# Moving the split of a streamed chunk later in the engines' order, in a kernel of Infini-attention beside a Fourier mixing layer

## The chip, the cores and the metric

The kernel runs on one core of one Trainium2 chip. The metric is the device time of one execution in microseconds (us). Three timed runs of the kernel before gave 1032.37, 1034.28 and 1035.39; the median is 1034.28.

## What is computed

Two independent layers, laid side by side in the output (2048 rows, 576 + 576 columns, float32):

```python
def _A_ref(x, wq, wk, wv, wo, beta):        # 32 heads of 18, 4 segments of 512
    ...
    for s in range(N):
        p = _softmax(qs @ ks^T * scale + mask)       # causal, inside the segment
        o = g * (phi(qs) @ M / (phi(qs) @ z)) + (1 - g) * (p @ vs)
        M, z = M + phi(ks)^T @ vs, z + sum(phi(ks))
    return o @ wo

def _B_ref(x, dft_seq_re, dft_seq_im, dft_hid_re, dft_hid_im):
    a = x @ dft_hid_re^T
    b = x @ dft_hid_im^T
    return dft_seq_re @ a - dft_seq_im @ b
```

(The first function is shortened to its mathematics.) The second layer, B, is the one that matters here: a product with a 576 x 576 matrix, and then one with a 2048 x 2048 matrix, once for the real and once for the imaginary part.

## The kernel before

To come near float32 in TensorE's fast formats, an operand is split into a high part and a low part: ScalarE copies it into the fast format (`hi`), and another engine subtracts that from the original (`lo`). A product is then hi·hi + hi·lo + lo·hi.

**Stages.** Up to about 230 us the projections of layer A run (L435 to L479). From there to about 960 us attention (`attention`, L811) and layer B (`dense`, L579) are woven together: attention is a list of slots, eight to each of 68 steps, and after every slot the loop at L879 takes pieces from the generator `dense` until layer B has come as far, by a planned share of time, as attention has. At each slot `tick` (L84) is called first; it runs what `later(n, ...)` (L81) has put off by n slots. The order in which instructions are written is the order in which each engine executes them: the schedule is manual, every engine takes its own list in order, and a waiting instruction holds up all behind it on its engine. From 960 us to the end there is the output projection (L899).

**Chunks of layer B.** The operands that layer B streams from memory come in 160 chunks (L369): for each of the two parts `ri`, 16 chunks of x (`xtT`, 128 x 640 values, one to each `hidden` at L536) and then 64 chunks of the 2048 x 2048 matrix (`cT`, 128 x 512 values, four to each `sequence` at L555). A chunk has three steps in its life:

- `c_load(n)` (L372): a DMA on SP's queue into `craw`, one of 4 buffers.
- `c_cut(n)` (L380): ScalarE writes `chi` (L387), for an x chunk also `xtail` (L389), from `craw` into one of 3 buffers; one slot later (L395) GpSimd writes `clo` (L392, and L394 for the tail). The first two chunks are cut in the stage before, with VectorE in GpSimd's place (L475).
- TensorE multiplies with `chi` and `clo` as weights: 28 matmuls to an x chunk (L545 to L550), 24 to a chunk of the matrix (L499).

`chunk(n)` (L531) is called when TensorE's order comes to chunk n. It issues the load of chunk n + 4 and the cut of chunk n + 2, and hands out the tiles of chunk n.

`sequence` walks through 16 steps `so`, four to a chunk. `product` (L495) takes the first two steps together, twelve steps singly, and the last two together again (`EDGE`, L493): a step's instructions written inside `steps` (L569) stand ahead of that step's matmuls.

**Others on the same queues.** On SP: loads of keys and queries (L426), the transposing DMA of the scores (L715), loads of y (L529). On ScalarE: the exponentials of the scores (L699, L754, L755), which also free the two pairs of PSUM banks that score matmuls (L670, L744 to L751) fill. On GpSimd: parts of the split of the exponentials (L710, L769), and the mask (L759).

Of the kernel before, what the change touches and what calls it, by code (L numbers as in the profile page):

```python
# [24 lines left out]
NT = S // P  # L25
# [11 lines left out]
def infini_attention_and_fnet(ctx: ExitStack, tc: tile.TileContext, xT, wqk, w8, wv, wo, beta, xtT, cT, hT, out):  # L37
# [15 lines left out]
    def split(hi, lo, raw, lo_engine=None):  # L53
        act.activation(hi, raw, AF.Copy)
        (lo_engine or dve).tensor_tensor(lo, raw, hi.bitcast(F32), OP.subtract)
# [25 lines left out]
    def later(n, fn, *a):  # L81
        due.setdefault(clock[0] + n, []).append((fn, a))
# [54 lines left out]
    def wide_tile(cols):  # L137
        return lambda: wide.tile([P, cols], F32R, name="wide", tag="wide")
# [233 lines left out]
    def c_load(n):  # L372
        if n < len(CHUNKS) and n not in c_seen:
            c_seen.add(n)
            src, at, k = CHUNKS[n]
            t = sr.tile([P, 5, P], F32, name="craw", bufs=4)
            dma(t[:, :k], src[at])
            c_raw[n] = t

    def c_cut(n, engine=pool):  # L380
        if n < len(CHUNKS):
            raw = c_raw.pop(n)
            hi = sr.tile([P, 4, P], F32R, name="chi", bufs=3)
            lo = sr.tile([P, 4, P], F32R, name="clo", bufs=3)
            t = sr.tile([P, P], F32R, name="xtail", bufs=3) if CHUNKS[n][2] == 5 else None
            c_split[n] = hi, lo, t
            act.activation(hi, raw[:, :4], AF.Copy)  # L387
            if t is not None:
                act.activation(t, raw[:, 4], AF.Copy)  # L389

            def low():
                engine.tensor_tensor(lo, raw[:, :4], hi.bitcast(F32), OP.subtract)  # L392
                if t is not None:
                    engine.tensor_tensor(t[64:], raw[64:, 4], t[64:].bitcast(F32), OP.subtract)  # L394
            later(1, low)  # L395
# [99 lines left out]
    def product(steps, count, evacuate):  # L495
        o = [ps.tile([P, 288], F32, name="d", bufs=3) for _ in range(2)]

        def mm(a, b, h, start=False, stop=False):
            pe.matmul(o[h], a, b[:, h * 288:h * 288 + 288], start=start, stop=stop)  # L499

        def edge(last):
            ops = [next(steps) for _ in range(EDGE)]
            for h in range(2):
                for n, (hi, lo, m_hi, m_lo) in enumerate(ops):
                    mm(hi, m_lo, h, start=n == 0 and not last)
                    mm(hi, m_hi, h)
                    mm(lo, m_hi, h, stop=n == EDGE - 1 and last)
                if last:
                    evacuate(h, o[h])
                yield 3 * EDGE * MM  # L510

        yield from edge(False)
        for _ in range(count - 2 * EDGE):
            hi, lo, m_hi, m_lo = next(steps)
            for h in range(2):
                mm(hi, m_lo, h)
                mm(hi, m_hi, h)
            yield 4 * MM
            for h in range(2):
                mm(lo, m_hi, h)  # L520
            yield 2 * MM
        yield from edge(True)
# [3 lines left out]
    def y_load(tt):  # L526
        if tt < NT:
            Y[tt] = sb.tile([P, D], F32, name="y", bufs=4)
            dma(Y[tt], yd[tt])  # L529

    def chunk(n):  # L531
        c_load(n + 4)
        c_cut(n + 2)
        return c_split.pop(n)

    def hidden(ri, tt):  # L536
        hi, lo = [(wide_tile(D)() if tt < 11 else sb.tile([P, D], F32R, name="ab", bufs=10)) for _ in range(2)]
        AB.append((hi, lo))
        xh, xl, xt = chunk(ri * 80 + tt)
        wh, wl, wt1, wt2 = HW[ri]  # L540
        for h in range(2):
            cs = slice(h * 288, h * 288 + 288)
            o = ps.tile([P, 288], F32, name="d", bufs=3)
            for k in range(4):
                pe.matmul(o, xh[:, k], wl[k][:, cs], start=k == 0, stop=False)  # L545
                pe.matmul(o, xh[:, k], wh[k][:, cs], start=False, stop=False)  # L546
                pe.matmul(o, xl[:, k], wh[k][:, cs], start=False, stop=False)  # L547
                yield 3 * HM
            pe.matmul(o, xt, wt1[:, cs], start=False, stop=False)
            pe.matmul(o, xt, wt2[:, cs], start=False, stop=True)  # L550
            split(hi[:, cs], lo[:, cs], o)
            yield 2 * HM
        yield BREAK

    def sequence(ri, tt):  # L555
        if ri:
            y_load(tt + 1)
            y = Y.pop(tt)
        else:
            y = sb.tile([P, D], F32, name="y", bufs=4)  # L560

        def evacuate(h, o):
            cs = slice(h * 288, h * 288 + 288)
            if ri == 0:
                act.activation(y[:, cs], o, AF.Copy)
            else:
                dve.tensor_tensor(y[:, cs], y[:, cs], o, OP.subtract)

        def steps():  # L569
            for so in range(NT):  # L570
                if so % 4 == 0:
                    hi, lo, _ = chunk(ri * 80 + NT + tt * 4 + so // 4)
                yield hi[:, so % 4], lo[:, so % 4], *AB[ri * NT + so]

        yield from product(steps(), NT, evacuate)
        later(2, dma, out[tt * P:(tt + 1) * P, D:] if ri else yd[tt], y)
        yield BREAK

    def dense():  # L579
        for ri in range(2):  # L580
            for tt in range(NT):
                yield from hidden(ri, tt)
            if ri:
                y_load(0)
            for tt in range(NT):
                late = tt - 8
                if ri == 0 and 0 <= late < 5:
                    h_load(1, late)
                if ri == 0 and 1 <= late < 6:
                    h_split(1, late - 1)  # L590
                if ri and 0 <= late < 5:
                    wo_load(late)
                if ri and 1 <= late < 6:
                    wo_split(late - 1)
                yield from sequence(ri, tt)
# [303 lines left out]
    for t in range(NT):  # L899
        o_transpose(t + 1)  # L900
        hi, lo, tl = OT.pop(t)
# [47 lines left out]
```

## Time and profile before

| | |
|---|---|
| timed runs, median | 1034.28 us (1032.37 to 1035.39) |
| the profiled execution: its time | 1032.0 us |
| its span, first to last instruction | 1030.3 us |
| granted TensorE clock | 1.0 |
| 235 to 960 us (attention and layer B) | where the changed lines run |
| `chi` (ScalarE, L387) | 160 of 632 ns (median) |
| `clo` on GpSimd (L392) | 158 of 1288 ns (median) |
| loads into `craw` (SP, L377) | 128 of 256 KB and 32 of 320 KB |

How to read what follows: PE is TensorE's matmuls, PEld its weight loads, DVE VectorE, ACT ScalarE, POOL GpSimd, SP the engine that issues the DMAs. In a list of waits, a row gives the waiting engine with what it writes and the line, what it waited for, and then the total in us, the number of times and the longest. In a timeline, a row gives start, duration, engine, line, operation, tiles and shapes, and in brackets how long the engine had stood idle and who ended that. Matmuls are pipelined, so that one lasts about 300 ns while the next starts 133 ns after it.

### The profile page before, as it was taken

What the parts mean: (1) busy time and instruction counts of PE and PEld (TensorE: products, weight loads), DVE (VectorE), ACT (ScalarE), POOL (GpSimd) and SP (SyncE); (2) the same over time, 40 slices, a digit from 0 to 9 for tenths busy, and PEclk for the clock granted to TensorE, in tenths of its full rate; (3) what the DMA queues carried; (4) which work ended last, traced back from release to release, by engine and by line L of the source; (5) the groups of instructions that cost most, each with busy time, mean ns of one, the idle gap of its engine ahead of it and who ended that gap; (6) DMA issues with size and microseconds to landing.
All of it is one profiled execution on the core that took longest, in us unless ns stands there. A gap on an engine that the chain in (4) does not pass through costs nothing.

```text
span 1030.3 us, 25826 instructions
## 1 busy us (share of the span) xinstructions
PE 1006.0 (98%) x9464; PEld 940.7 (91%) x9464; DVE 719.8 (70%) x1903; ACT 713.7 (69%) x1654; POOL 625.3 (61%) x668
## 2 busy tenths in 40 slices
PE   9999999999999999999999999999999999999998
PEld 7989989899999999999998999998899888899998
DVE  6545657465678777778778777778688778896442
ACT  7657575653887878878877787876677767875333
POOL 3557575766666666767667676666566666766000
PEclk9999999999999999999999999999999999999999
DMA  7516253377768999999999988899999999968574
GB/s 265 172 65 201 88 166 145 130 234 186 166 155 195 197 211 196 213 187 211 235 192 216 207 199 165 163 211 197 205 221 214 220 217 210 243 150 192 155 209 138
DMA packets 287263, 194.26 MB, mean 189 GB/s; under 512 B 210208, under 2 KB 242336, under 8 KB 287136
## 3 DMA queue, kind: packets, MB, share of 16 engines
q1 hardware_dynamic: 287136, 192.61, 79.2%
q8 instruction: 74, 1.21, 0.5%
q14 instruction: 53, 0.43, 0.1%
HBM read 106.64 MB, written 43.78 MB: 146 GB/s over the span
## 4 chain that ended last, share of the span: by engine, by line
PE 69%; DMA 11%; ACT 6%; SPq 6%; POOL 5%; issue 2%; DVE 1%; POOLq 0%; ACTq 0%; DVEq 0%
PE d L499 21%; DMA craw<-cT 8%; PE qk L77 6%; PE d L77 6%; PE v L77 5%; PE qk L229 5%; PE s L670 4%; PE d L545 3%; PE d L546 3%; PE d L547 3%; POOL clo L392 3%; SPq L715 2%; PE pv L786 2%; SPq L87 2%; PE look L338 2%
## 5 line engine op out<-in xcount | busy, mean ns | idle before, releaser
L676 DVE CUSTOM_DVE_ANT_0 s<-s,causal 128x128 f32<-128x128 f32 (+3 forms) x512 | 251.2, 499 | 109.9 <-PE s L670 95.3
L392 POOL TENSOR_TENSOR clo<-craw,chi 128x512 fp32r<-128x512 f32 x158 | 214.1, 1356 | 125.5 <-ACT chi L387 80.4
L499 PE MATMUL d<-wide,chi 128*128 128x288 f32 x1408 | 266.5, 306 | 0.0
L499 PEld LDWEIGHTS d<-wide,chi 128*128 128x128 f32 x1408 | 212.3, 189 | 3.3 <-issue 2.2
L499 PE MATMUL d<-wide,clo 128*128 128x288 f32 x704 | 178.1, 319 | 0.0
L710 POOL TENSOR_TENSOR hl<-pf,hl 128x768 f16<-128x768 f32 x64 | 111.5, 1742 | 77.8 <-ACT hl L706 57.9
L387 ACT ACTIVATE chi<-craw 128x512 fp32r<-128x512 f32 x160 | 100.9, 631 | 63.4 <-DMA craw<-cT 40.6
L670 PE MATMUL s<-ks,qs 108*128 108x128 bf16 (+3 forms) x512 | 133.9, 304 | 10.5 <-ACT pf L699 8.4
L699 ACT ACTIVATE pf<-s,nb 128x128 f32<-128x128 f32 (+3 forms) x256 | 128.1, 526 | 6.2
L499 PE MATMUL d<-ab,chi 128*128 128x288 f32 x640 | 126.1, 306 | 0.0
L499 PEld LDWEIGHTS d<-wide,clo 128*128 128x128 f32 x704 | 119.0, 189 | 1.8 <-issue 0.9
L769 DVE TENSOR_TENSOR plo<-pf,phi 128x384 f16<-128x384 f32 (+1 forms) x128 | 110.9, 867 | 0.2
L754 ACT ACTIVATE phi<-t 128x384 f16<-128x384 f32 x128 | 62.1, 485 | 66.3 <-PE t L751 66.2
L499 PEld LDWEIGHTS d<-ab,chi 128*128 128x128 f32 x640 | 98.5, 189 | 4.4 <-issue 4.0
L755 ACT ACTIVATE pf<-t 128x384 f32<-128x384 f32 (+1 forms) x192 | 99.9, 520 | 1.3 <-PE t L744 1.3
L706 ACT ACTIVATE hl<-pf 128x768 f16<-128x768 f32 (+1 forms) x128 | 87.4, 730 | 2.0
L499 PE MATMUL d<-ab,clo 128*128 128x288 f32 x320 | 84.9, 314 | 0.0
L545 PE MATMUL d<-wide,chi 128*128 128x288 f32 x256 | 84.3, 329 | 0.0
L546 PE MATMUL d<-wide,chi 128*128 128x288 f32 x256 | 75.6, 295 | 0.0
L547 PE MATMUL d<-wide,clo 128*128 128x288 f32 x256 | 75.5, 295 | 0.0
L710 DVE TENSOR_TENSOR hl<-pf,hl 128x512 f16<-128x512 f32 x64 | 72.1, 1127 | 1.8 <-ACT hl L706 1.8
L769 POOL TENSOR_TENSOR plo<-pf,phi 128x384 f16<-128x384 f32 x64 | 62.4, 976 | 11.1 <-ACT pf L755 10.6
(196 smaller groups left out, 2510.4 us busy)
## 6 DMA issues: line engine op xcount, KB each, us to landing
craw<-cT SPq DMA_DIRECT2D x128, 256.0 KB
ks<-kd SPq DMA_DIRECT2D x192, 72.0 KB
qs<-qd SPq DMA_DIRECT2D x192, 72.0 KB
craw<-xtT SPq DMA_DIRECT2D x32, 320.0 KB
out<-y SPq DMA_DIRECT2D x31, 288.0 KB
vd<-vs SPq DMA_DIRECT2D x16, 440.0 KB
vst<-vd SPq DMA_DIRECT2D x32, 220.0 KB
qd<-p SPq DMA_DIRECT2D x16, 384.0 KB
```

Source lines behind the costliest of these rows:

```text
L77: pe.matmul(o, a, b, start=n == 0, stop=n == len(terms) - 1)
L387: act.activation(hi, raw[:, :4], AF.Copy)
L392: engine.tensor_tensor(lo, raw[:, :4], hi.bitcast(F32), OP.subtract)
L499: pe.matmul(o[h], a, b[:, h * 288:h * 288 + 288], start=start, stop=stop)
L545: pe.matmul(o, xh[:, k], wl[k][:, cs], start=k == 0, stop=False)
L546: pe.matmul(o, xh[:, k], wh[k][:, cs], start=False, stop=False)
L547: pe.matmul(o, xl[:, k], wh[k][:, cs], start=False, stop=False)
L670: pe.matmul(o[:, c:c + w], q[:, i * P:w], k[:, :w], start=True, stop=True)
L676: dve.tensor_tensor_reduce(o[:, c:c + w], o[:, c:c + w], CAUSAL[0][:, L - w:], scale=scale, scalar=-LOWEST, op0=OP.add, op1=OP.min, accum_ ...
L699: act.activation(f[:, FIRST_COL[i]:FIRST_COL[i] + w], o[:, c:c + w], AF.Exp, bias=nb[:, i:i + 1], scale=-1.0)
L710: engine.tensor_tensor(hl[:, 1, a:b], f[:, a:b], hl[:, 0, a:b], OP.subtract)
L769: (pool if kind == 2 else dve).tensor_tensor(lo[:, a:b], f[:, a:b], hi[:, a:b], OP.subtract)
```

## The change

The cut of chunk n + 2 no longer stands in `chunk(n)`. In `hidden` it is written after the first half of the chunk (14 of 28 matmuls and the split of their result); in `sequence` it is written when the chunk's fourth step is taken. The load of chunk n + 4 stays in `chunk(n)`. `c_cut` itself, the number of buffers and all amounts of work are as before.

```diff
     def chunk(n):
         c_load(n + 4)
-        c_cut(n + 2)
         return c_split.pop(n)
...
             split(hi[:, cs], lo[:, cs], o)
+            if h == 0:
+                c_cut(ri * 80 + tt + 2)
             yield 2 * HM
...
             for so in range(NT):
+                n = ri * 80 + NT + tt * 4 + so // 4
                 if so % 4 == 0:
-                    hi, lo, _ = chunk(ri * 80 + NT + tt * 4 + so // 4)
+                    hi, lo, _ = chunk(n)
+                if so % 4 == 3:
+                    c_cut(n + 2)
                 yield hi[:, so % 4], lo[:, so % 4], *AB[ri * NT + so]
```

## The prediction

> **What bounds the kernel now.** I read the page's busy shares first, then the busy time by stretch, then the waits of TensorE, and then the two lines that the change moves.
>
> ```profile
> PE 1006.0 (98%) x9464; PEld 940.7 (91%) x9464; DVE 719.8 (70%) x1903; ACT 713.7 (69%) x1654; POOL 625.3 (61%) x668
> ```
>
> TensorE is the bound, and 1030.3 - 1006.0 = 24.3 us of the span is its idle time. No change to ScalarE or GpSimd can win more than that unless matmuls get denser. The stretches say where the idle time is (columns: window, length, busy us and count of PE, PEld, DVE, ACT, POOL, granted clock, DMA share, GB/s):
>
> ```profile
> 300.00:400.00 100.00, 99.28 (x1088) 93.01 (x1088) 77.87 (x228) 78.49 (x187) 67.45 (x73) 1.00 0.93 196
> ...
> 500.00:600.00 100.00, 96.92 (x1048) 90.49 (x1047) 78.53 (x220) 78.53 (x189) 68.95 (x70) 1.00 0.96 208
> 600.00:700.00 100.00, 99.98 (x1047) 94.36 (x1046) 76.83 (x233) 78.71 (x196) 67.35 (x80) 1.00 0.91 182
> 700.00:800.00 100.00, 95.43 (x1038) 89.17 (x1037) 77.94 (x227) 72.54 (x170) 63.64 (x66) 1.00 0.97 212
> 800.00:900.00 100.00, 94.02 (x1012) 87.46 (x1011) 80.60 (x222) 73.45 (x167) 66.77 (x69) 1.00 1.03 223
> ```
>
> 300-400 and 600-700 have under 1 us of idle TensorE; 500-600 has 3.1, 700-800 4.6, 800-900 6.0. From 235 to 960, where the changed lines run, it comes to 17.5 us. TensorE's own waits name who ends it; these are all of them in 232-960:
>
> ```profile
> PE s L670 <- ACT pf L699: 8.4, 10, 1.6
> PE t L747 <- ACT pf L699: 3.4, 4, 1.5
> PE trm L727 <- ACT pf L755: 1.8, 4, 0.7
> PE s L670 <- DVE negm L676: 1.6, 2, 0.9
> PE t L744 <- DMA qs<-mt: 1.5, 1, 1.5
> ```
>
> ScalarE's exponentials (L699, L755) free the score banks that TensorE wants next: 8.4 + 3.4 + 1.8 = 13.6 us. The 1.5 us on the maxima's DMA is ScalarE's too: the tile `mt` is written by ScalarE (L729). Together 15.1 us. ScalarE is busy only 73-79% in these stretches, so it is late because it was blocked, and the moved line says by what (idle time of ScalarE just before `chi`, and who waited for `chi`):
>
> ```profile
> its engine sat idle before it (us, times) until:
>   DMA craw<-cT: 40.6, 29
>   DMA craw<-xtT: 8.3, 3
>   PE t L744: 7.0, 2
>   PE d L499: 3.6, 6
>   PE t L751: 1.7, 1
>   PE pv L787: 1.0, 1
>   issue: 0.7, 1
> who waited for it (us, times):
>   POOL clo L392: 80.4, 65
> ```
>
> The sum is 62.9 us. One case from the timelines of ScalarE and TensorE:
>
> ```profile
> 711.42 0.63 ACT L387 ACTIVATE chi<-craw 128x512 fp32r<-128x512 f32 x1 [4.50 <-DMA craw<-cT]
> ...
> 714.42 0.69 ACT L699 ACTIVATE pf<-s,nb 128x512 f32<-128x512 f32 x1
> ```
> ```profile
> 714.35 0.38 PE L670 MATMUL s<-ks,qs 108*128 108x512 bf16 x1 [1.52 <-ACT pf L699]
> ```
>
> The load of this chunk is issued on SP at 706.83, and `chi` waits for it until 711.4. Exponentials stand behind it in ScalarE's order, and TensorE stops 1.52 us for one of them. I went through the 19 gaps of TensorE in 235-960 that are put to ScalarE or to `qs<-mt`: all but one (0.70 us, at 922.7) have such a wait of `chi` in the 5 us before them. So **14.4 of the 17.5 us** of idle are the price of `chi` waiting for its load in ScalarE's queue.
>
> **The change, part by part.** No instruction is added or removed: 160 `chi` (L387, 632 ns median), 32 `xtail`, 158 `clo` on GpSimd (L392, 1288 ns median) stay. Only their place in the two queues moves. The loads are issued at the same place in SP's order, so SP's queue (192 `ks`, 192 `qs`, 160 `craw`, 64 transposes and the rest) keeps its order.
>
> *How far it moves.* In the trace's order a cT chunk has 24 main matmuls of TensorE. The split moves from ahead of the first to ahead of the 19th; in the last chunk of a row (steps 14 and 15 are fetched together, L502) to ahead of the 13th. In an xtT chunk it moves to behind the 14th of 28. By the trace's times of those matmuls: 3.2, 2.2 and 2.0 us, median of all 3.0. In the xtT chunk it also stands behind ScalarE's evacuation of the first half (L551, 0.41 us a piece), which waits for that 14th matmul; `clo` of the chunk two ahead keeps 2.7 us or more there once the start is over, so this costs nothing. A cT chunk lasts 4.5 us, an xtT chunk 4.9.
>
> *The load's lead.* Where `chi` waited, it started 4.6 us (median) after its load was issued. From the load's issue to TensorE reaching the old place there are 5.5 us in the median, and under 4.6 us in 54 of 153 chunks (the first seven left out). To the new place there are 8.3 us, and under 4.6 us in 6 of 153, short by 4.2 us in all six together. A wait of `chi` under about 1 us is followed by no gap on TensorE. I take 1 us of TensorE's 14.4 as left: **-13.4 us**. Bounds: 0, if a later load always eats the lead, and -15.1, all of ScalarE's.
>
> [...]
>
> *The wait for TensorE.* `chi` of chunk n+2 takes the buffer of chunk n-1 (3 buffers, L383). At the head of chunk n that chunk has only just ended (`PE d L499: 3.6, 6`); 3 us on it has long ended. Nothing waits on that 3.6 us but ScalarE, so I count no gain beyond the above.
>
> *What is shortened: the lead of `clo` before TensorE.* From the head of chunk n to the end of `clo` of n+2 takes 3.7 us in the median (ScalarE's lag, 0.63 us of `chi`, the tick to the next slot, 1.3 us of `clo`); the first matmul that reads it comes 9.7 us after the head. That leaves 5.9 us. Taking away each chunk's own shift leaves 3.0 us in the median. If each lag is kept as it was, waits for loads included, only two chunks fall short: chunk 2 by 0.6 us, chunk 54 by 0.02. If lags of chunks without a load wait are set against all leads, the shortfall sums to 1.0 us. I take **+1.6 us** (1.0 and chunk 2's 0.6). Bounds: 0, and for the other end see the first rival. TensorE's waits of before show `PEld d L499 <- POOL clo L392` just once (1.2 us).
>
> *Buffers of the load.* The load of n+4 reuses the buffer that `clo` of n releases (4 buffers, L376). It is issued at least 3.5 us after that release now; with the shift at least 0.3, median 6.1. SP gets no new wait, and what stands behind it (transposes, `ks`, `qs`) is not held up. Price 0; if SP ran ahead of its place by more than 6 us, a load would wait and with it the transposes.
>
> *What is late next.* Each `chi` wait also holds up GpSimd's `clo` (80.4 us, 65 times), the score split behind it, and SP's transpose, which waits 84.0 us for `clo`; behind that transpose stands the next load (the load at 706.83 was issued right after a transpose that had held SP 3.9 us). Removing the wait loosens that loop; I count nothing for it. VectorE is at 77-81% and holds TensorE up only twice (1.6 us).
>
> Sum: -13.4 + 1.6 = **-11.8 us** on the profiled 1032.0 us, so 1020.2. The profiled run lies 2.3 us under the median of the three timed runs, 1034.28; from that the change gives 1022.5. I predict **1022.5**.
>
> **The rivals.**
>
> *Slower: TensorE waits for `clo`.* The 3.0 us left for `clo` must cover all that GpSimd has ahead of it. If the new place falls such that each `clo` stands behind one more score split (L710, 1742 ns), the leads of the trace fall short by 21 us in all; at 1.36 us more lag they fall short by 12.7, which is the turning point against 13. Then 1034.3 - 13.4 + 21 = 1042. For it: 61% busy on GpSimd, and a lag that can't be seen at the new place. Against it: chunk heads already fall at all phases of the slots, so the lags seen now contain such queues, and 32 of them hold a load wait that goes.
>
> [...]
>
> *The wait moves on, half the gain.* With `chi` out of the way ScalarE's next waits or VectorE's score minima set the banks, as in the two gaps put to VectorE. If half of the 13.4 comes back, the time is 1034.3 - 6.7 + 1.6 = 1029.
>
> *The transfers are the bound.* The DMA share is 0.96-1.03 just where TensorE idles and 0.91-0.93 where it doesn't. If loads are late because the engines are full, a longer lead fills up again and nothing is won: 1034. Against it: 600-700 runs without idle TensorE at 0.91, so the loads' pace suffices there with little to spare, and the waits are single ones of up to 4.5 us behind a held SP queue, not a lag that grows.
>
> *It doesn't do what it says:* the split would have to stay ahead of the chunk's first matmul in ScalarE's order; nothing in the code makes it.
>
> **How the numbers follow.** Forecast (1015 to 1028) 0.62; half the gain (1026 to 1032) 0.14; transfers or no effect (1032 to 1037) 0.09; slower by late `clo` (1037 to 1055) 0.15. The range takes in the first two, the bound of -15.1 with the denser loop behind it, and most of the third: 1014 to 1035, leaving out 0.15 above and a few hundredths below. About 0.3% (3 us) is what a measurement of this kernel can tell from no change. Faster 0.76, same 0.09, slower 0.15.
>
> **What would show it.** Right: idle before `chi` until `craw` falls from 48.9 us to under 10; TensorE's waits for ScalarE in 235-960 from 13.6 to under 3; 700-900 gets busier than 98%. Wrong: new rows of TensorE waiting for `clo` of more than 5 us; `chi` still waiting for `craw` 20 us or more (transfers the bound); or the `chi` wait gone with TensorE's idle unchanged under another name.

## The result, and the profile after

The changed kernel takes **1025.50 us** in the median of nine runs (1023.30 to 1032.20); the kernel before, timed beside it, 1032.37 us (nine runs). The ratio is **0.9939, with a 95% interval of 0.9913 to 0.9966**: by that ratio 6.3 us faster on 1034.28 us, where 11.8 us were forecast (the two medians, 1032.37 and 1025.50, differ by 6.9). The changed kernel's two profiles below were taken in executions of 1032.2 and 1027.0 us.

The first profile is thus of the slowest of the nine executions, with a span (first to last instruction) of 1030.5 us. The second (`e1_again`, below) has a span of 1025.3 us; its execution is 1.5 us above the median. Both are read here, since what differs between them is part of the answer.

First ScalarE's idle time just before `chi`, from the view of that line in the first profile after:

```profile
its engine sat idle before it (us, times) until:
  DMA craw<-cT: 14.0, 9
  PE d L499: 5.4, 3
  DMA craw<-xtT: 3.2, 1
  POOL mb L726: 2.0, 1
```

The waits for the load fell from 48.9 us in 32 waits to 17.2 us in 10: the change does what it says. But the waits that are left are longer, up to 6.1 us against 4.5. Rows of this view that name an engine which writes nothing that `chi` reads should be counted with them: for the chunks of `PE t` and `PE pv` before (9.6 us, 4 times), and of `POOL mb` and two of `PE d` after (4.9 us, 3 times), the load had been issued 3.9 to 6.3 us before `chi` began, as in the rows that name it, and the buffer of `chi` had been free for 1.1 to 5.0 us. By that count, an estimate, the waits for loads went from 58.5 us to 22.1, and to 18.0 in the second profile. TensorE's own waits in 232-960, same profile:

```profile
PE s L674 <- ACT pf L703: 7.4, 3, 4.6
PE t L748 <- DMA qs<-mt: 6.3, 6, 1.9
PE s L674 <- DVE negm L680: 1.1, 3, 0.7
...
```

In the second profile the first two are:

```profile
PE s L674 <- ACT pf L703: 6.6, 3, 2.8
PE t L748 <- DMA qs<-mt: 4.8, 3, 2.3
```

(L674, L703, L748 and L680 are L670, L699, L744 and L676 of before.) The waits for ScalarE's exponentials went from 18 short ones, 13.6 us, to three, 7.4 us. The DMA that brings the scores' maxima (`qs<-mt`, two transfers of 3 KB), waited for once before, 1.5 us, now costs 6.3. And the stretches show something new in the column behind the five engines, the granted clock:

```profile
700.00:800.00 100.00, 96.69 (x1048) 90.18 (x1044) 79.37 (x228) 74.42 (x172) 66.54 (x68) 1.00 0.99 212
800.00:900.00 100.00, 93.46 (x981) 87.36 (x980) 76.79 (x219) 70.02 (x161) 62.03 (x67) 0.95 1.00 219
```

In stretches of 10 us the place is seen:

```profile
830.00:840.00 10.00, 5.42 (x42) 5.13 (x41) 3.73 (x10) 4.64 (x10) 3.97 (x3) 0.66 1.03 180
...
870.00:880.00 10.00, 10.00 (x99) 9.35 (x98) 7.15 (x24) 6.19 (x17) 4.23 (x8) 0.83 1.01 201
```

TensorE had half its clock for 6.8 us from 832.8 and for 3.4 us from 870.4. The first lies inside and behind its longest stop, the second behind the stop of 1.88 us for the maxima's DMA that ended at 869.0. In 870-880 TensorE is busy throughout and still does 99 matmuls, where 820-830 holds 111. The profile of before has no such stretch from 235 to 960.

The longest stop, from the timelines of SP, ScalarE and TensorE of the same profile:

```profile
818.87 4.12 SPq L719 DMA_TRANSPOSE ptt<-hl  x1
...
828.45 0.36 SPq L377 DMA_DIRECT2D craw<-cT  x1
```
```profile
833.44 0.63 ACT L387 ACTIVATE chi<-craw 128x512 fp32r<-128x512 f32 x1 [6.13 <-DMA craw<-cT]
```
```profile
834.72 0.58 PE L674 MATMUL s<-ks,qs 108*128 108x128 bf16 x2 [4.58 <-ACT pf L703]
```

SP issues two loads of chunks 10.1 us apart (818.33 and 828.45), where TensorE at full pace uses one every 4.5 us: between them stand the transposing DMA and eight other issues. The split, though late, comes too early for that load; ScalarE stops 6.1 us and TensorE 4.6.

Adding up what TensorE's time went into (idle time in 235-960 from its gaps; half of the time at half clock, an estimate of the work lost in it: in the first profile after, L499's matmuls start 240 ns apart (median) in these stretches, and 133 ns apart at full clock from 840 to 850; the rest of the span):

| profile | span | idle | lost to half clock | rest |
|---|---|---|---|---|
| before | 1030.3 | 17.5 | 0 | 1012.8 |
| after | 1030.5 | 16.0 | 5.1 | 1009.4 |
| after, again | 1025.3 | 12.7 | 3.4 | 1009.2 |

So the idle time of 5.7 us that I expected (17.5 - 13.4 + 1.6) is 12.7 to 16.0, and 3.4 to 5.1 us go to the clock by that estimate. The rest falls by some 3.5 us: the stop of before at 714.35 cost some 0.16 us beyond its idle time (it puts 1.68 us more than usual between two starts, of which 1.52 are idle), and there are 27 stops of more than 0.06 us before, 17 and 11 after; if each cost as much, that is, by estimate, 1.6 to 2.6 us of it.

### The profile page after: what moved, and what is told of

Its sections match the earlier page's. It is cut to its first block, busy times and chain, and to the rows that moved or that the text cites. A ratio compares the mean times of both kernels' runs of the same rounds, so it can differ in the third digit from the quotient of the medians.

```text
span 1030.5 us, 25808 instructions
## 1 busy us (share of the span) xinstructions
PE 1008.0 (98%) x9464; PEld 943.8 (92%) x9464; DVE 724.8 (70%) x1903; ACT 714.6 (69%) x1654; POOL 624.8 (61%) x668
## 4 chain that ended last, share of the span: by engine, by line
PE 80%; DMA 8%; ACT 5%; DVE 3%; POOL 2%; issue 1%; SPq 1%; POOLq 0%; DVEq 0%; ACTq 0%
PE d L499 33%; PE s L674 6%; PE d L77 6%; PE qk L77 5%; PE qk L229 4%; PE v L77 4%; PE pv L790 4%; DMA qs<-mt 3%; PE d L544 2%; PE d L545 2%; PE d L546 2%; PE pv L791 2%; PE m L313 2%; PE look L338 1%; DMA ks<-kd 1%; PE t L748 1%
## 5 line engine op out<-in xcount | busy, mean ns | idle before, releaser
L680 DVE CUSTOM_DVE_ANT_0 s<-s,causal 128x128 f32<-128x128 f32 (+3 forms) x512 | 250.8, 500 | 112.1 <-PE s L674 98.8
L392 POOL TENSOR_TENSOR clo<-craw,chi 128x512 fp32r<-128x512 f32 x158 | 211.0, 1336 | 123.3 <-ACT chi L387 86.1
L499 PE MATMUL d<-wide,chi 128*128 128x288 f32 x1408 | 268.0, 307 | 0.0
L499 PEld LDWEIGHTS d<-wide,chi 128*128 128x128 f32 x1408 | 213.6, 190 | 2.6 <-issue 1.6
L499 PE MATMUL d<-wide,clo 128*128 128x288 f32 x704 | 178.7, 320 | 0.0
L714 POOL TENSOR_TENSOR hl<-pf,hl 128x768 f16<-128x768 f32 x64 | 115.9, 1811 | 70.6 <-ACT hl L710 59.2
L674 PE MATMUL s<-ks,qs 108*128 108x128 bf16 (+3 forms) x512 | 134.6, 305 | 9.2 <-ACT pf L703 7.4
L703 ACT ACTIVATE pf<-s,nb 128x128 f32<-128x128 f32 (+3 forms) x256 | 128.3, 527 | 6.2
L499 PE MATMUL d<-ab,chi 128*128 128x288 f32 x640 | 126.7, 307 | 0.0
L499 PEld LDWEIGHTS d<-wide,clo 128*128 128x128 f32 x704 | 119.6, 190 | 0.9
L773 DVE TENSOR_TENSOR plo<-pf,phi 128x384 f16<-128x384 f32 (+1 forms) x128 | 113.8, 889 | 0.0
L759 ACT ACTIVATE pf<-t 128x384 f32<-128x384 f32 (+1 forms) x192 | 100.4, 523 | 8.5 <-PE t L748 8.4
L499 PEld LDWEIGHTS d<-ab,chi 128*128 128x128 f32 x640 | 99.4, 190 | 0.4
L499 PE MATMUL d<-ab,clo 128*128 128x288 f32 x320 | 85.6, 317 | 0.0
L714 DVE TENSOR_TENSOR hl<-pf,hl 128x512 f16<-128x512 f32 x64 | 75.2, 1175 | 0.1
L773 POOL TENSOR_TENSOR plo<-pf,phi 128x384 f16<-128x384 f32 x64 | 59.7, 933 | 16.8 <-ACT pf L759 15.9
```

Source lines behind the costliest of these rows:

```text
L674: pe.matmul(o[:, c:c + w], q[:, i * P:w], k[:, :w], start=True, stop=True)
L680: dve.tensor_tensor_reduce(o[:, c:c + w], o[:, c:c + w], CAUSAL[0][:, L - w:], scale=scale, scalar=-LOWEST, op0=OP.add, op1=OP.min, accum_ ...
L703: act.activation(f[:, FIRST_COL[i]:FIRST_COL[i] + w], o[:, c:c + w], AF.Exp, bias=nb[:, i:i + 1], scale=-1.0)
L714: engine.tensor_tensor(hl[:, 1, a:b], f[:, a:b], hl[:, 0, a:b], OP.subtract)
L759: act.activation(f[:, r:r + w], o[:, :w], AF.Exp, bias=LIFT, scale=SCALE)
L773: (pool if kind == 2 else dve).tensor_tensor(lo[:, a:b], f[:, a:b], hi[:, a:b], OP.subtract)
```

## The experiments

Theory A, formed on these profiles: the gain is the load's lead, as forecast, and its remainder is eaten by the clock and by the maxima's DMA, which is a matter of order in the queues. Against it B (the clock is chance), C (the gain comes from the new place of the split on ScalarE and GpSimd and not from the load), D (the transfers are the bound) and E (the maxima's DMA is only a symptom). Each ratio is against the kernel before, run on the same chip in the same rounds.

**The changed kernel again** (no edit).

> The changed kernel once more, for a second profile and its clock. Theory A (the change takes chi's wait for its load, 48.9 us, down to about 17 us, and the rest of the expected gain is eaten by a half clock of TensorE after its longest waits and by new waits for the maxima's DMA): 0.993 to 0.995 of the kernel before; granted clock below 1 again, with each stretch at 0.5 right behind an idle time of TensorE of about 2 us or more; TensorE's waits for the maxima's DMA again above the 1.5 us of before. Rival B (the profiled run was an odd one; the clock has nothing to do with the change): the clock stands at 1.000 and the time at 0.989, as predicted.

Measured: 0.9940 (0.9919 to 0.9961). The mean granted clock of its nine runs is 0.9969; that of 32 runs of the kernel before is 0.9985. (1 - clock) times the span, the same estimate of the work lost, is 3.2 us against 1.5. By it some 1.7 us of the forecast gain went to the clock in the mean of the timed runs. B falls: none of the changed kernel's eighteen timed runs stands at 1.000, and the time is not 0.989.

**The load one chunk earlier, the split left at the head.**

```diff
     def chunk(n):
-        c_load(n + 4)
+        c_load(n + 5)
         c_cut(n + 2)
```

> The kernel before with the load issued one chunk earlier (chunk n loads n + 5 in place of n + 4) and the split left at the head. Theory A (what the change wins is the load's lead before chi): the lead grows by a whole chunk, 4.5 us, more than the change's 3.0 us, so chi's waits for craw fall below 10 us and the time to 0.988 to 0.993. Rival C (the gain comes from where the split stands in the order of ScalarE and GpSimd, not from the load's lead): 0.998 to 1.002. Rival D (the transfers are the bound): chi's waits stay above 30 us and the time within 0.3% of before.

Measured: 0.9953 (0.9931 to 0.9976), 1025.36 us in the median. `chi`, and then TensorE:

```profile
  DMA craw<-xtT: 4.2, 3
...
  DMA craw<-cT: 0.9, 1
```
```profile
PE t L744 <- DMA qs<-mt: 8.2, 6, 4.0
```

C falls: nearly the same gain comes without moving the split. D falls in the form it had here: `chi`'s waits did not stay above 30 us. But A misses its range too (0.988 to 0.993): the waits for the load are down to 5.1 us and the time is no better than with 17.2 us of them. The maxima's DMA has taken their place, with a stop of 4.0 us and 6.8 us of half clock that set in during it. In that case ScalarE had written the maxima at 832.5, SP came to their DMA at 838.2, behind a transpose and ten other issues, and TensorE went on at 843.2. So of 10.7 us, 5.7 were spent in SP's order and 5.0 after SP had come to the DMA, for 6 KB.

**Only one part of the change.** In `hidden` or in `sequence` the three lines of the old `chunk` are put back at the chunk's head:

```diff
-        xh, xl, xt = chunk(ri * 80 + tt)
+        c_load(ri * 80 + tt + 4)
+        c_cut(ri * 80 + tt + 2)
+        xh, xl, xt = c_split.pop(ri * 80 + tt)
...
-            if h == 0:
-                c_cut(ri * 80 + tt + 2)
```

(This is `e3_sequence_only`, which undoes the change in `hidden`; `e2_hidden_only` undoes it in `sequence` in the same way.)

> Only the sequence part of the change (cT chunks split late, in the fourth step; in hidden the split stays at the chunk's head). Theory A: 40.6 of the 48.9 us of waits for craw and all but two of TensorE's gaps behind such a wait lie in the cT chunks, so this has nearly the whole gain: 0.993 to 0.996. Rival C (gain spread by the number of chunks, 128 of 160): 0.995 to 0.997.

Measured: 0.9950 (0.9931 to 0.9969), inside what A and C both allow.

> Only the hidden part of the change (xtT chunks: the split behind the first half). Theory A: 8.3 us of wait for craw in three waits lie there, and TensorE lost about 1 us behind one of them (586 us); 0.998 to 1.001. Rival: by the number of chunks (32 of 160) 0.998 to 0.999, which this cannot tell apart; above 1.003 the later clo in hidden costs something.

Measured: 0.9992 (0.9966 to 1.0018). The gain is in `sequence`, where 40.6 of the 48.9 us of waits for loads were. The interval takes in both rivals' numbers; that nothing is lost in `hidden` is shown, within 0.2%.

**A shorter lead still.** The split of chunk n + 1 at the head of chunk n:

```diff
     def chunk(n):
         c_load(n + 4)
+        if n:
+            c_cut(n + 1)
...
-            if h == 0:
-                c_cut(ri * 80 + tt + 2)
...
-                if so % 4 == 3:
-                    c_cut(n + 2)
```

> The changed kernel with the split later still: that of chunk n + 1 at the head of chunk n, a lead of 1.0 chunks and not 1.25. The rival of the prediction (TensorE waits for clo): the median lead of clo falls from 3.0 to about 1.4 us, the turning point; by the leads of the trace the shortfalls then sum to some 13 us, so rows of TensorE waiting for clo or chi of 8 to 20 us and 1.000 to 1.012 of before. If leads under 3 us are harmless (the lags at the later place are shorter, since the load has landed by then): 0.992 to 0.996.

Measured: 0.9965 (0.9945 to 0.9986), 1028.22 us. TensorE's waits:

```profile
PE t L746 <- DMA qs<-mt: 4.6, 2, 2.7
PE d L499 <- POOL clo L392: 3.0, 4, 1.0
...
PE d L499 <- ACT chi L387: 0.8, 2, 0.6
```

Here the forecast's first rival appears, at less than half of the least that was expected: 3.8 us of waits for `clo` and `chi`, not 8 to 20. In this kernel `chi` waits for a load once, 0.2 us. So the leads of the trace of before overstated the risk, and a lead of 1.25 chunks is not short in this kernel.

**The maxima's DMA.** Three ways to have it earlier. First their transpose a slot earlier, on the changed kernel and on the load-early one:

```diff
+            if p % 2 == 0 and 0 < p <= NP:
+                maxima_transpose(p // 2 - 1)
             even(0, s_fill, 1)
...
-            if p % 2 == 0 and 0 < p <= NP:
-                maxima_transpose(p // 2 - 1)
             even(V_LAG, pv)
```

> The changed kernel with the transpose of the maxima, and so its two DMAs, one slot (some 1.3 us) earlier. Theory A (what ate the rest of the gain are TensorE's waits for the maxima's DMA, 4.8 and 6.3 us in two profiles of the changed kernel, and the half clock behind the longest of them): those waits fall below 3 us, and the time to 0.989 to 0.992 of the kernel before. Rival E (the maxima's DMA is a symptom: it is late because everything on SP is late behind the transposing DMAs, and something else will wait): the waits for it fall but the time stays at 0.993 to 0.995.

Measured: 1.0035 (1.0015 to 1.0055), 1037.19 us.

> The kernel before with the load issued one chunk earlier, the split left at the head, and the maxima's transpose one slot earlier. Theory A: chi waits for craw under 10 us as in the load-early kernel, and TensorE's waits for the maxima's DMA under 3 us (8.2 there): 0.987 to 0.991, granted clock 0.998 or more. Rival E: 0.994 to 0.996 as the load-early kernel alone.

Measured: 1.0050 (1.0030 to 1.0069). Both miss what either theory said, by a mistake in the experiment: the transpose needs a PSUM bank that ScalarE has not yet read at that slot. TensorE's waits in the changed kernel with this edit:

```profile
PE trm L731 <- ACT pf L759: 15.8, 10, 6.0
...
PE t L748 <- DMA qs<-mt: 0.5, 1, 0.5
```

The wait for the DMA is gone (0.5 us), and a new one, of TensorE for ScalarE's exponentials (L759), is larger than what it cured. They tell A and E apart no further. Second, the two DMAs issued by ScalarE:

```diff
-            later(1, dma, qs_bufs[G % 4][NPAIR:NPAIR + 3, 2 * h]...
+            act.dma_start(qs_bufs[G % 4][NPAIR:NPAIR + 3, 2 * h]...
```

> The changed kernel with the maxima's two DMAs issued by ScalarE right behind the copy that makes their source, not by SP a slot later. Theory A: their wait in SP's order (5.7 us in one case of the load-early kernel) is gone, so TensorE's waits for them vanish; ScalarE pays 64 issues of 0.7 us or so, 45 us over 700, at 75% busy. If the issues are cheap for ScalarE: 0.988 to 0.992; if they push the exponentials back: 0.995 or more, with new waits of TensorE for ScalarE. Rival E: 0.993 to 0.995 as the changed kernel.

Measured: 1.0055 (1.0033 to 1.0078). TensorE no longer waits for the maxima, and 64 issues of 0.75 us have left SP; but `chi`, and TensorE behind ScalarE and behind the transposed scores, wait more than in the changed kernel:

```profile
  DMA craw<-cT: 35.4, 22
```
```profile
PE s L674 <- ACT pf L703: 10.0, 5, 3.7
PE pv L790 <- DMA ptt<-hl: 7.3, 9, 2.1
```

Third, the DMAs in SP's order at once:

```diff
-            later(1, dma, qs_bufs[G % 4][NPAIR:NPAIR + 3, 2 * h]...
+            dma(qs_bufs[G % 4][NPAIR:NPAIR + 3, 2 * h]...
```

> The changed kernel with the maxima's two DMAs written into SP's order at once and not a slot later, their transpose staying where it is. Theory F: TensorE's waits for them fall under 3 us, but chi's waits or those for the transposed scores grow; time 0.992 to 0.997. Theory A: the waits fall and nothing takes their place: 0.988 to 0.991, and this would be a version that beats both.

Measured: 0.9950 (0.9934 to 0.9967). The waits for the maxima fall to 3.9 us, `chi` still waits 17.4 us for loads, and no time is won over the changed kernel. The interval leaves out what A said (0.988 to 0.991).

**Both leads**, the split late and the load early:

```diff
     def chunk(n):
-        c_load(n + 4)
+        c_load(n + 5)
         return c_split.pop(n)
```

> The changed kernel with the load issued one chunk earlier too (chunk n loads n + 5), so that chi has 3.75 chunks from issue to split. Theory F: chi's waits for craw are gone (under 3 us), TensorE's waits for the maxima's DMA are 6 us or more, time 0.992 to 0.997. Theory A: 0.990 to 0.993. A load now takes a buffer that clo frees only some 1.5 us before in program order; if SP gets to it first it waits there with everything behind it: 0.998 or more.

Measured: 0.9948 (0.9920 to 0.9976). `chi` waits for no load at all, and the time is that of the changed kernel once more. TensorE's waits:

```profile
PE t L748 <- DMA qs<-mt: 8.8, 4, 3.8
```

SP did wait here for buffers, 18.4 us before 15 loads (each issued within 0.13 us of the end of the `clo` that frees its buffer), but none of the four stops follows within 40 us of one. The changed kernel, the load-early one, the one with the maxima at once and this one have each cured other waits, and they all end between 0.9939 and 0.9953. That leads from rivals D and E to theory F: what SP and the transfers can deliver in 400-600 and 700-900 sets the pace, and a cure at one place moves the wait to another. One test of it was left out: no run has the load early and the maxima's DMAs at once, so it is not shown that curing both waits by order alone would win nothing.

**Less to deliver.** The test of F: the transposing DMA of the odd heads' scores cut to half, on either kernel. Only the high part is transposed, and the value product takes it in the low part's place, so the low part's share of those heads is left out of the result.

```diff
-        nc.sync.dma_start_transpose(PT[n], hl.rearrange("p a c -> p (a c)"))
+        nc.sync.dma_start_transpose(PT[n][:, :10], hl[:, 0])
...
-                    hi, lo = pt[:, b], pt[:, 10 + b]
+                    hi, lo = pt[:, b], pt[:, b]
```

> The changed kernel with the transposing DMA of the odd heads' scores cut to half: only the high part is transposed, and the value product uses it in place of the low part, so the matmuls stay and the low part of those heads is left out of the result. The 64 transposes hold SP some 3.9 us each (252 us) and are a large part of the transfers. Theory F (what SP and the transfers can deliver is the bound in 400-600 and 700-900; each cure at one place moves the wait to another): with both relieved, chi's waits for craw and TensorE's for the maxima's DMA fall to under 5 us together, no half clock in 235-960, and 0.983 to 0.988 of the kernel before. Theory A (the waits are matters of order in the queues): the transposes still stand ahead of the loads, so waits of over 8 us stay: 0.989 to 0.993.

Measured: **0.9812 (0.9790 to 0.9834)**, 1012.24 us.

> The kernel before with the same halved transposes. Theory F: chi's waits for craw fall from 48.9 us to under 15 without moving the split, and the time to 0.984 to 0.990, within 0.4% of the changed kernel with halved transposes: with supply enough the change is worth little. Theory A: chi at the head still waits 25 us or more, the time is 0.993 to 0.997, and the change is still worth 0.5% or more on top.

Measured: **0.9832 (0.9810 to 0.9853)**, 1014.21 us. The kernel before, its split still at the head, with halved transposes; first the stretches, then `chi`, then the two largest of TensorE's waits in 232-960 (two more are 0.2 us each):

```profile
700.00:800.00 100.00, 100.00 (x1096) 93.96 (x1095) 81.36 (x241) 75.61 (x174) 69.30 (x72) 1.00 0.89 189
800.00:900.00 100.00, 99.92 (x1097) 93.65 (x1097) 85.58 (x238) 77.43 (x177) 69.59 (x72) 1.00 0.87 195
```
```profile
  DMA craw<-xtT: 6.2, 2
...
  DMA craw<-cT: 1.4, 1
```
```profile
PE s L670 <- DVE negm L676: 1.6, 2, 0.9
PE trm L727 <- ACT pf L755: 0.7, 1, 0.7
```

The waits for loads fall from 48.9 to 7.6 us without moving anything, the maxima's DMA is waited for no more, TensorE's idle time is 2.9 us, and the clock stays at 1.000. With the change on top the idle time is 1.4 us and the time 2.0 us less (four runs of each, which do not overlap: 1011.73 to 1012.86 and 1014.15 to 1014.62). So of the 6.3 us that the change is worth with full transposes, 2.0 stay and some 4 are won only while the transposes are full. F's waits came out as it said, and both times below its ranges; A's numbers (25 us or more of waits at the old place, 0.989 to 0.997) are refuted.

What this does not settle is why the full transposes made the loads late. The edit relieves three things at once. The transfers: the DMA share in 700-800 falls from 0.99 to 0.88 between the changed kernel and its halved form. SP's time: it is inside an instruction 66% of 700-800 there, not 87% (worked out from its records), and its issues of the transposes shrink, the first line being the changed kernel's and the second its halved form's:

```profile
L719 SPq DMA_TRANSPOSE ptt<-hl x64: 3022/3898/5987, 267.6 to 942.8; - x64
```
```profile
L719 SPq DMA_TRANSPOSE ptt<-hl x64: 1287/1540/2419, 262.0 to 920.0; - x64
```

And the order: a load behind one transpose waits 2.4 us less, and the halved transpose no longer waits for the low part. 23 of the 64 are issued before that is written, on either kernel, up to 4.3 us before; of the full ones none is. SP's idle time just before the transposes falls from 38.4 to 16.5 us on the kernel before and from 30.6 to 13.8 on the changed one. The lead from a load's issue to the old place grows from 5.5 us to 8.2 in the median, by little more than the shorter issue alone. So a form of theory A in which each load is late behind one long issue fits these two runs as well as F does.

That taking 64 issues off SP (`e12_maxima_from_act`) made the loads later, with transposes of 4.2 us in the median, speaks against the number of SP's issues as the bound; but SP also stood idle 59.0 us just before its transposes there, so later sources had a part in it. It was not tried to relieve the transfers, SP's time or the order alone.

## Why the prediction was right or wrong

The direction, the place and the cause of the gain were right; its size was not. 1025.5 us lies in the range, only 3.0 us from the forecast, but that nearness is in part luck: the kernel before, timed beside it, ran at 1032.37 us and not at 1034.28. The gain is 6.3 us where 11.8 were forecast, and the interval (3.5 to 9.0 us of 1034.3) leaves that out.

- *What bounds the kernel.* Right: `chi` at the chunk's head held up ScalarE, and ScalarE TensorE. The load-early kernel wins nearly the same by the load alone (0.9953 against 0.9940 in the same rounds).
- *The load's lead, -13.4 us.* **This is the step that failed.** It took SP's issue times as fixed against TensorE. In the trace of before the lead to the new place was 8.3 us in the median and under 4.6 us in 6 of 153 chunks; in the two profiles after it is 7.4 and 8.0 us, and under 4.6 in 17 and 10, short by 17.6 and 11.1 us together and not by 4.2. To the old place the lead shrank too, from 5.5 us to 4.6 and 5.0. TensorE moved forward and SP's issues did not follow as far; why not is open, as said above. Of the 14.4 us of waits 1.0 should have been left; ScalarE's exponentials and the maxima's DMA still cost 13.7 and 11.4 us. TensorE's idle time fell by 1.5 and 4.8 us, not by 13.4.
- *The transfers as the bound*, my third rival at 0.09, was set aside too easily. I set against it that 600-700 runs without idle TensorE at a DMA share of 0.91. That shows that 0.91 suffices, and not that 0.97 does; with halved transposes 700-900 runs at 0.87 to 0.89 and TensorE hardly stops. Whether the transfers are what was short is not shown, and the time did not stay at 1034.
- *The clock was not in the sum.* With fewer but longer stops (up to 4.58 and 2.8 us in the profiles after, where before has none over 1.61 from 235 to 960) came half-clock stretches: by the estimate above some 1.7 us in the mean of the timed runs, 5.1 and 3.4 us in the profiles.
- *What is late next.* I named the score banks and VectorE. It was the maxima's DMA (1.5 us before, 4.8 and 6.3 after), which I had counted among ScalarE's waits because ScalarE writes its source.
- *SP's transposes* I read as waiting 84.0 us for `clo`. That was wrong: in both kernels none of the 64 was issued before its two sources were written, and the 3 to 6 us are the issue itself. The view names an engine that happened to signal meanwhile. Read rightly, SP spends 252 us inside these 64 issues, which would have spoken for a short supply. The same fault lies in four of the 19 gaps that I went through: the waits of `chi` ahead of them (3.0 and 3.9 us) stand in the rows of `PE t L744`. Their loads were issued 4.7 and 6.3 us before, so the reading of the gaps holds.
- *`clo`'s lead, +1.6 us.* It cost nothing: TensorE waits for `clo` in neither profile after. By my count of leads 3.0 us should have been left in the median; 4.2 were.
- *The buffers of the load:* as forecast, no wait of a load for its buffer shows; the nearest one is issued 0.23 us after its buffer came free.

Of the signs I named, `chi`'s idle time went to 17.2 us, neither under 10 nor over 20 (22.1 by the wider count, which would have been a sign for the transfers); TensorE's waits for ScalarE to 7.4, not under 3; 700-900 to 95%, not over 98. Half a cure everywhere fits a shared shortage, but does not prove one.

## What to carry to other kernels

A lead that is read from a trace need not hold once the consumer runs faster: before counting a wait as won, see whether the queue that feeds it (here SP, inside instructions 83 to 90% of each 100 us from 300 to 900 except 600-700, with DMA shares of 0.90 to 1.03) could keep pace. When several cures of different waits all end at the same time, look for what they share, and test it by taking away some of the load; and check what else that edit takes away (here it also freed the transposes of a wait). And rows that name a releaser should be checked against when the real source was ready.

## What the runs showed of the hardware

**Stops of TensorE and its clock.** From the 14 profiles, all stops over 1.2 us from 235 to 955 and whether half clock set in at them (from 2.5 us before the stop ended to 1.5 us after it):

| idle time of the stop | stops | with half clock |
|---|---|---|
| 1.24 to 1.77 us | 27 | 0 |
| 1.83 to 1.97 us | 11 | 5 |
| 2.10 to 5.96 us | 13 | 13 |

A half-clock stretch lasted 3.41 us (13 times) or 6.83 us (5 times): 1.7 or 3.4 us of work on top of the stop, by the estimate above. None of the 18 set in anywhere else. In the first profile after, the stop of 4.58 us that ended at 834.72 had 6.83 us of half clock from 832.85, and the stop of 1.88 us that ended at 868.99 had 3.41 us from 870.39.

In the first profile after, a third half-clock stretch, at the kernel's end, begins at 1030.82; the second and the third begin 37.54 and 197.97 us behind the first, 11 and 58 times 3.413 us. What parts the five stops of the middle row that had half clock from the six that had none is not shown.

In these runs, then, one stop of 4 us cost more than the same idle time in stops of 1.24 to 1.77 us: the stops of 3.81 and 4.04 us came with 3.41 and 6.83 us of half clock, those 27 with none. The first profile after shows what joining short stops into longer ones can cost this kernel: 1.5 us less idle time than before, and 5.1 us lost to half clock by the estimate.

**A transposing DMA on SP** held its queue 3.0 to 6.0 us for 128 x 2560 two-byte values (median 3.9) in the first profile after and 1.5 us (median) for half of that in `e13_half_transpose_after`, against 0.37 us (median) for the plain 256 KB load in the first profile after. Behind it, two transfers of 3 KB were what TensorE waited for, 4.0 us in `e5_load_early`.
